# Attention with a gated feed-forward block: one shifted array of the bit-made exponentials goes from VectorE to GpSimd, with a new rule for the number of summed groups

## The chip, the cores and the metric

The kernel runs on one core of a Trainium2 chip. The metric is the device time of one execution in microseconds (us). Three runs of the kernel before gave 769.53, 769.68 and 769.78 us, a median of 769.68.

Five engines matter. TensorE (PE) multiplies matrices into the PSUM banks. ScalarE (ACT) computes the exact exponentials. VectorE (DVE) evicts PSUM banks and makes a second kind of exponential. GpSimd (POOL) has some clearing to do at the start and then rests. SyncE (SP) issues most of the transfers.

## The reference

```python
g = sigmoid((x * gate_w).sum(-1, keepdims=True))       # x: 2048 x 512
q, k, v = split(x @ wqkv)                              # 32 heads of 16
p = softmax(q @ k.T * 16 ** -0.5)                      # 2048 x 2048 for each head
a = concat(p @ v) @ wo
b = (silu(x @ w_gate) * (x @ w_up)) @ w_down           # 1792 columns between
out = g * a + (1 - g) * b
```

The bulk of it is the softmax: 32 heads of 2048 x 2048 exponentials.

## The kernel before

**Tiles.** A unit is 512 queries of four heads; there are 32 of them, and each meets 16 tiles of 128 keys. That makes 512 tiles, numbered n. A tile is four score matrices of 128 keys x 512 queries, one for each head of the unit.

**Two ways to an exponential.** A tile that goes to ScalarE (`emit_pair`, L704) takes two pairs: TensorE writes two heads' scores into a two-bank buffer `s_t` (there are two of these buffers), ScalarE's Exp reads them and writes `e_t`, 128 x 1024 in bf16. A tile that goes to VectorE (`emit_d`, L774) is made from bits. TensorE writes one head's scores into a bank `d_t`; where it can, that matmul runs beside a score pair of ScalarE's ("riding"). VectorE evicts the bank with one multiply and one add into 16-bit integers (`first`, L788). Those integers, read as bf16, are a piecewise linear approximation of the exponential. Four evictions fill an array `c_t` of 128 x 2048 for the four heads; call it y.

**Two corrections.** The approximation is evened out in one of two forms, and `groups[n]` says which. With two groups, VectorE makes two arrays from y with bit operations (`bits`, L825) and multiplies one of them by y (`product`, L834). With four groups, VectorE makes three more arrays by adding 25, 56 and 94 to the integers of y (`SHIFTS`, `copy`, L817). The softmax sum then runs over all arrays of the tile, so that TensorE does the product with V ("PV", `pv`, L902) once for each group: two or four times for a tile of VectorE's, once for a tile of ScalarE's. A PV group is four matmuls that stand side by side in the array, one a head, all into the accumulator `o_ps`.

**Where the arrays live.** Seven places ("homes", `NS`) hold the arrays y and their shifted or masked copies: six tiles of the pool `vex`, and a seventh that is room in `wd_t` early and in `kaug` later. `take_home` picks the one that comes free first, `drop` gives it back once its last reader is planned.

**Around it.** The projections, the feed-forward block and the output products are cut into pieces that TensorE takes between the score pairs.

**What sets the order.** The program is written out by a planner in Python, as it is built. It keeps a clock for TensorE, VectorE and ScalarE (`plan.pe`, `plan.dve`, `plan.act`), adds assumed costs, and always emits the work that fits next. Each engine then runs its instructions strictly in that order (`ordered`, L152), and semaphores hold it where data is late. `v_unit` (L1444) and `v_take` (L1461) decide when VectorE takes a tile away from the end of the unit; ScalarE has the rest (`hi[un]`). `quad` (L1469) decides on two or four groups: two where fewer than two homes are free, four where TensorE had spare time (`spare`) or where `EAGER` holds, else two. Before, `EAGER` never holds. Margins of the plan are constants: `m_free` (L361) lets a bank be reused 0.2 us after its planned eviction, and `d_wait` (L807) plans an eviction 0.28 us after its matmul.

Of the kernel before, what the change touches and what calls it, by code (L numbers as in the profile page):

```python
# [9 lines left out]
ALU = mybir.AluOpType  # L10
AX = mybir.AxisListType
BF16 = mybir.dt.bfloat16
F32 = mybir.dt.float32
U16 = mybir.dt.uint16
# [65 lines left out]
def kernel(  # L80
# [12 lines left out]
    nc = tc.nc  # L93
    P = 128
# [9 lines left out]
    KT = S // P  # L104
    QBW = 512
    QB = S // QBW
# [11 lines left out]
    NV = 4  # L118
    NS = 7
# [5 lines left out]
    SHIFTS = (25.0, 56.0, 94.0)  # L125
# [15 lines left out]
    vex = ctx.enter_context(tc.tile_pool(name="vex", bufs=1))  # L141
# [21 lines left out]
    def mm(*args, **kw):  # L163
        return ordered(nc.tensor.matmul(*args, **kw))  # L164
# [12 lines left out]

    vec = Ordered(nc.vector)
    queue = Ordered(nc.sync)


    xT = big.tile([P, DC, S], BF16, name="xT")
    wd_t = big.tile([P, FC, D], BF16, name="wd_t")
# [36 lines left out]
    kaug = big.tile([P, G, S], BF16, name="kaug")  # L220
# [66 lines left out]


    class Plan:
        pe = dve = act = 0.0  # L290
        mode = last = None
        seq = 0
        slot = -1
# [2 lines left out]
    plan = Plan()  # L296
    owed = []
    work_at = []
    banks = [0.0] * 3
    held = [None] * 3  # L300

    def spend(mode, mms, ready=0.0):

        plan.seq += 1
        work_at.append((plan.pe, mms))
        plan.pe = max(plan.pe + (FLIP if mode != plan.mode else 0.0), ready) + (0.226 if mode == "F" else 0.217) * mms
        plan.mode = mode
# [40 lines left out]
    def m_tile(name, ride=None):  # L348
        while m_ready() is None:
            stuck()  # L350
        i = min((i for i in range(3) if banks[i] is not None), key=lambda i: banks[i])
        if ride is None:
            plan.pe = max(plan.pe, banks[i])
        else:
            ride.append(max(plan.pe - ROUND, banks[i]) + ROUND)
            plan.pe = max(plan.pe, ride[0])
        banks[i] = None
        held[i] = ps_m[i].tile([P, QBW], F32, tag=f"m{i}", name=name)
        return held[i]

    def m_free(ps, t):  # L361
        i = [h is ps for h in held].index(True)
        banks[i], held[i] = t + 0.2, None

    def emit_piece(c):
        mms, f = c.pieces[c.i][:2]
# [313 lines left out]
    c_free = [0.0] * NS  # L680
# [3 lines left out]
    vready = []  # L684
# [15 lines left out]
    e_end = {}  # L700
# [38 lines left out]
    d_wait = []  # L739
# [9 lines left out]
    def drop(i, t):  # L749
        u = users[i]  # L750
        u[:] = u[0] - 1, max(u[1], t)
        if not u[0]:
            c_free[i] = u[1]

    def take_home():
        i = min(range(NS), key=lambda i: c_free[i])
        t, c_free[i] = c_free[i], 1e9
        assert t < 1e9
        users[i] = [1, 0.0]
        return i, t  # L760

    def home(i=None, t=0.0):

        if i is None:
            i, t = take_home()
        plan.dve = max(plan.dve, t)
        if i < NS - 1:
            return i, vex.tile([P, NV * QBW], U16, tag=f"h{i}", name="c_t", bufs=1)[:, :]
        return i, (kaug[:, 0, :] if au > QB else wd_t[:, 0:4, :].rearrange("p f d -> p (f d)")).bitcast(U16)

    ROUND = 0.217
    BANK_WAIT = 0.2
# [1 line left out]
    def emit_d(i, rows=32, riding=False):  # L774
        if not vcur:
            n = v_take()
            waiting[n] = [NV, None, take_home()]
            vcur.update(n=n, left=list(range(NV)), y=None)
            y_live[0] += 1
        n, left, cur = vcur["n"], vcur["left"], waiting[vcur["n"]]  # L780
        left.remove(i)
        end = []
        d_t = m_tile("d_t", end if riding else None)
        score(d_t[:, :], 4 * n + i, rows)
        if not left:
            vcur.clear()

        def first():  # L788
            if cur[1] is None:
                cur[1] = home(*cur[2])  # L790
            h, y = cur[1]
            vec.tensor_scalar(out=y[:, i * QBW:(i + 1) * QBW], in0=d_t[:, :], scalar1=EXP_A, scalar2=EXP_B[groups[n]],
                              op0=ALU.mult, op1=ALU.add)
            m_free(d_t, plan.dve)
            cur[0] -= 1
            if cur[0]:
                return
            plan.last = ("y", n)
            if groups[n] == 2:
                vops.extend([(0.6, lambda: bits(n, 0, y), ("y", n), n, True), (0.6, lambda: bits(n, 1, y), None, n, True),  # L800
                             (MUL_US, lambda: product(n, h, y), None, n, False)])
            else:
                users[h][0] = 2
                ready(n, 0, h, y)
                for k in range(1, 4):
                    vops.append((0.6, lambda k=k: copy(n, k, h, y), ("y", n) if k == 1 else None, n, True))
        d_wait.append(((end[0] if end else plan.pe) + 0.28, first, n))  # L807

    waiting = {}
    copies = {}  # L810
    part = {}

    def ready(n, k, h, c):
        copies[n, k] = (c.bitcast(BF16), h)
        vready.append((plan.dve + 0.3, n, k))

    def copy(n, k, i, y):  # L817
        h, c = home()
        vec.tensor_scalar(out=c, in0=y, scalar1=SHIFTS[k - 1], scalar2=None, op0=ALU.add)
        ready(n, k, h, c)  # L820
        if k == 3:
            drop(i, plan.dve + 0.2)
            y_live[0] -= 1

    def bits(n, k, y):  # L825
        h, c = home()
# [75 lines left out]
    def pv(n, k=None, most=QBW):  # L902

        un = n // KT
        c0 = cut.pop("done", 0)
        c1 = min(QBW, c0 + most)
        cols = slice(c0, c1)
        if un not in o_of:
            while un and un - 1 not in osbs:
                pay()  # L910
            plan.pe = max(plan.pe, o_end[0])
            o_of[un] = ps_o.tile([P, QBW], F32, tag="o", name="o_ps")
        if v_of(n) is not None:
            force(v_of(n))
        o = o_of[un]
        first = pvs[un] in ((0, KT // 2) if un == 0 else (0,))
        last = un == 0 and pvs[un] == KT // 2 - 1 or pv_left(un) == 1
        if k is not None:
            c, slot = copies[n, k]
        for i, b in enumerate(range(4 * n, 4 * n + 4)):  # L920
            j = HEADS[i]
            v0 = (4 * UNIT[un][1] + j) * VC
            e = e_of[b] if k is None else c[:, i * QBW:(i + 1) * QBW]
            mm(o[32 * j:32 * j + 32, cols], lhsT=vaug[:, n % KT, v0:v0 + 32], rhs=e[:, cols],
               start=first, stop=last, tile_position=(0, 32 * j), skip_group_check=True)
        share = (c1 - c0) / QBW
        if c1 < QBW:
            cut.update(item=(n,) if k is None else (n, k), done=c1)
            spend("C", share, 0.0 if k is not None else max(e_end[b] for b in range(4 * n, 4 * n + 4)))
            return  # L930
        cut.clear()
        if k is not None:
            copies.pop((n, k))
        else:
            for b in range(4 * n, 4 * n + 4):
                e_of.pop(b)
                e_left.pop(b, None)
        pvs[un] += 1
        if un == 0 and pvs[0] == KT // 2:
            later(0.6, take_part, plan.pe + 0.47)  # L940
        spend("C", share, 0.0 if k is not None else max(e_end.pop(b, 0.0) for b in range(4 * n, 4 * n + 4)))
        if k is None:
            done_a[un] += 1
        else:
            done_v[un] += 1
            drop(slot, plan.pe + 0.2)
# [187 lines left out]

    plan.act = plan.pe
    plan.dve = plan.pe + 3.9


    pace = Pacer()
# [57 lines left out]
    def v_of(n):  # L1197

        return v_rest[n - QB * KT] if QB * KT <= n < QB * KT + KT else None
# [4 lines left out]
    for qb in range(1, QB):  # L1204
        d = qb * KT
        q, bd = q0_pieces(qb)
        q = pace.add(q, 0, d - 13, [known])
# [3 lines left out]
    for qb in range(QB):  # L1211
        for b in range(NB):
            d = UNIT.index((qb, max(2 * b, 1))) * KT
# [17 lines left out]
            q = pace.add(q_pieces(qb, b), rel, d - QLEAD, after)  # L1231
# [16 lines left out]
    for pos, qb in enumerate(ORDER):  # L1248
# [13 lines left out]
        for tq in range(TQ):  # L1262

            def cond(qb=qb):
                return qb == QB - 1 or all((qb, b) in normed for b in range(NB))
            rel = 100 if pos == 0 else (UNIT.index((qb, G - 1)) + 1) * KT + 16
            c = pace.add((out_pieces if pos else down_pieces)(qb, tq), rel, a0 + per * (0.64 + 0.36 * (tq + 1) / TQ),
                         (gus if tq == 0 else prev) + gates, cond=cond)
# [10 lines left out]
    au = at_ = half = begun = 0  # L1279
    vu = 0  # L1280
    hi = [KT] * UNITS
# [155 lines left out]
    TILE_US = 1.9  # L1437
# [23 lines left out]
    def v_take():  # L1461
        un = v_unit()
        hi[un] -= 1
        n = un * KT + hi[un]
        groups[n] = 2 if quad() else 4
        forward()
        return n

    def quad():  # L1469
        if sum(f < 1e9 for f in c_free) < FREE4:  # L1470
            return True
        if spare[0] > SPARE or EAGER(len(GQL()), back[0]):
            spare[0] = 0.0
            return False
        return True
    FREE4 = 2
    EAGER = lambda q, b: False
    GQL = lambda: []
    back = [0]

# [10 lines left out]
    while au < UNITS:  # L1491
# [10 lines left out]
        if room > 0.02:  # L1502
# [3 lines left out]
            c = side(room + SLACK)  # L1506
# [30 lines left out]
        n = au * KT + at_  # L1537
# [7 lines left out]
    while closed < UNITS or vops or vcur:  # L1545
# [9 lines left out]
        c = side(2.0)  # L1555
# [20 lines left out]
    un = UNITS - 1  # L1576
# [17 lines left out]
    for tq in range(TQ):  # L1594
        t = (QB - 1) * TQ + tq
# [39 lines left out]
```

## Time and profile before

| | us or count |
|---|---|
| median of three runs | 769.68 |
| the profiled execution's own time | 769.63 |
| its span, first to last instruction | 767.9 |
| busy: PE / DVE / ACT / POOL | 733.1 / 738.8 / 752.5 / 10.6 |
| Exp of pairs on ScalarE | 780 (390 tiles) |
| evictions of `d_t` on VectorE | 488 (122 tiles) |
| passes over 128 x 2048 integers on VectorE | 288 |
| products over 128 x 2048 on VectorE | 78 |

780 pairs are 390 tiles of ScalarE's; 488 evictions are the other 122. Of these, 78 have two groups (each has two passes and a product) and 44 have four (three passes each): 2 x 78 + 3 x 44 = 288 passes. The groups of rows in the profile are split by the name of the buffer, so that passes and evictions that write to or read from the seventh home appear under `kaug` or `wd_t`. The mean duration of a row counts each instruction from its start to its end; consecutive instructions overlap, so the busy time divided by the count is the better price of one more. All three big engines are busy for over 95% of the span. The granted clock of TensorE is 1.000 throughout.

### The profile page before, as it was taken

How to read it: one execution, taken by the hardware profiler on the slowest of the kernel's cores; microseconds unless marked ns; L12 is line 12 of the kernel's file. 1: busy time of each engine (PE TensorE's matmuls, PEld its weight loads, DVE VectorE, ACT ScalarE, POOL GpSimd, SP SyncE). 2: the span in 40 equal slices, each digit the busy share in tenths (PEclk: the TensorE clock that was granted, in tenths of full speed). 3: DMA queues.
4: the chain of work that ended last, by engine and by line, in shares of the span. 5: the costliest groups of instructions: out<-in, count | busy, mean ns of one | idle time of the engine just before them, and what ended most of it. 6: DMA issues, size and time to landing. Idle time of an engine off the chain costs nothing.

```text
span 767.9 us, 22047 instructions
## 1 busy us (share of the span) xinstructions
PE 733.1 (95%) x9044; PEld 221.6 (29%) x9045; DVE 738.8 (96%) x1213; ACT 752.5 (98%) x849; POOL 10.6 (1%) x25
## 2 busy tenths in 40 slices
PE   8999999999999999999999999999999999999997
PEld 3323222222222222223322222223222322222222
DVE  6889999999999999999999999999999999999994
ACT  5999999999999999999999999999999999999996
POOL 5000000000000000000000000000000000000000
PEclk9999999999999999999999999999999999999999
DMA  8002304134200113220100230311000232100001
GB/s 192 2 5 50 73 15 85 31 107 101 57 19 13 32 24 78 60 52 22 37 26 12 49 84 20 75 34 41 20 12 26 60 77 59 31 16 16 16 28 35
DMA packets 91020, 34.38 MB, mean 45 GB/s; under 512 B 75488, under 2 KB 90472, under 8 KB 90920
## 3 DMA queue, kind: packets, MB, share of 16 engines
q1 hardware_dynamic: 89192, 32.66, 17.8%
q8 instruction: 70, 1.15, 0.6%
q10 hardware_dynamic: 1728, 0.33, 0.2%
q14 instruction: 30, 0.25, 0.1%
HBM read 21.55 MB, written 2.35 MB: 31 GB/s over the span
## 4 chain that ended last, share of the span: by engine, by line
ACT 32%; PE 30%; DVE 28%; issue 8%; DMA 1%; SPq 1%; DVEq 0%; ACTq 0%
ACT e_t L167 30%; DVE c_t L176 17%; PE s_t L164 10%; PE o_ps L164 8%; PE gu L164 6%; DVE kaug L176 3%; PE ops L164 3%; DVE mt L176 2%; DVE gs L176 2%; ACT th L167 1%; DVE on L176 1%; PE qp L164 1%; DVE osb L176 1%; PE warm L164 1%; SPq L176 1%
## 5 line engine op out<-in xcount | busy, mean ns | idle before, releaser
L167 ACT ACTIVATE e_t<-s_t 128x1024 bf16<-128x1024 f32 x780 | 728.3, 1105 | 1.3 <-PE s_t L164 0.7
L176 DVE TENSOR_SCALAR c_t<-d_t 128x512 uint16<-128x512 f32 x420 | 275.3, 681 | 2.2 <-PE d_t L164 2.0
L164 PE MATMUL s_t<-qx,kaug 32*128 32x512 bf16 (+1 forms) x1228 | 239.0, 384 | 16.1 <-ACT e_t L167 14.0
L164 PEld LDWEIGHTS <-kaug 32*128 32x128 bf16 (+1 forms) x2048 | 88.7, 91 | 321.8 <-issue 317.6
L164 PE MATMUL o_ps<-e_t,vaug 128*32 128x512 bf16 (+2 forms) x1608 | 154.2, 379 | 0.0
L176 DVE TENSOR_SCALAR c_t<-c_t 128x2048 uint16<-128x2048 uint16 x212 | 142.0, 683 | 1.7 <-PE o_ps L164 1.4
L164 PE MATMUL d_t<-qx,kaug 32*128 32x512 bf16 x404 | 131.9, 383 | 0.0
L164 PE MATMUL o_ps<-c_t,vaug 128*32 128x512 bf16 (+2 forms) x1244 | 111.3, 370 | 2.6 <-DVE osb L176 2.1
L164 PEld LDWEIGHTS <-vaug 128*32 128x32 bf16 x3048 | 68.8, 94 | 107.2 <-issue 95.2
L164 PE MATMUL gu<-xT,wg 128*32 128x512 bf16 x896 | 73.0, 384 | 0.0
L164 PE MATMUL gu<-xT,wu 128*32 128x512 bf16 x896 | 68.3, 382 | 0.2 <-DVE c_t L176 0.2
L176 DVE TENSOR_TENSOR c_t<-c_t 128x2048 bf16<-128x2048 bf16 x50 | 60.7, 1213 | 0.0
L164 PE MATMUL ops<-wd_t,mt 128*32 128x512 bf16 x672 | 57.5, 382 | 0.0
L164 PE MATMUL s_t<-q,kaug 32*128 32x512 bf16 (+1 forms) x196 | 38.2, 383 | 5.8 <-ACT e_t L167 5.4
L176 DVE TENSOR_SCALAR kaug<-d_t 128x512 uint16<-128x512 f32 x60 | 39.6, 680 | 0.0
L176 DVE SCALAR_TENSOR_TENSOR mt<-gs,gu 128x512 bf16<-128x512 bf16 x56 | 38.1, 680 | 1.5
L176 DVE SCALAR_TENSOR_TENSOR gs<-th,gu 128x512 bf16<-128x512 bf16 x56 | 38.0, 678 | 0.5 <-ACT th L167 0.5
L167 ACT ACTIVATE th<-gu 128x512 bf16<-128x512 f32 x56 | 37.7, 673 | 0.0
L164 PEld LDWEIGHTS <-mt 128*32 128x32 bf16 (+1 forms) x1037 | 24.5, 95 | 28.6 <-issue 22.0
L164 PEld LDWEIGHTS <-wu 128*32 128x32 bf16 x896 | 19.5, 95 | 25.4 <-issue 17.6
L164 PEld LDWEIGHTS <-wg 128*32 128x32 bf16 x896 | 17.8, 94 | 26.0 <-issue 23.2
L176 DVE TENSOR_SCALAR kaug<-c_t 128x2048 uint16<-128x2048 uint16 x33 | 22.5, 681 | 0.1
(141 smaller groups left out, 444.7 us busy)
## 6 DMA issues: line engine op xcount, KB each, us to landing
wg<-in_B_w_gate_dram SPq DMA_DIRECT2D x56, 128.0 KB
wu<-in_B_w_up_dram SPq DMA_DIRECT2D x56, 128.0 KB
on<-osb SPq DMA_DIRECT2D x120, 16.0 KB
rb<-rr SPq DMA_DIRECT2D x15, 128.0 KB
wd_t<-in_B_w_down_dram SPq DMA_DIRECT2D x7, 256.0 KB
qx<-qst SPq DMA_DIRECT2D x96, 16.0 KB
qx<-aq SPq DMA_DIRECT2D x96, 16.0 KB
out_dram<-o_t SPq DMA_DIRECT2D x12, 128.0 KB
```

Source lines behind the costliest of these rows:

```text
L164: return ordered(nc.tensor.matmul(*args, **kw))
L167: ordered(nc.scalar.activation(*args, **kw))
L176: return lambda *a, **kw: ordered(f(*a, **kw))
```

## The change

For a tile of four groups, the planner now asks `g_fits` whether the third shifted array (the one with 94 added) can be made by GpSimd. It can when GpSimd's own planned clock `plan.pool` is at most 2.0 us ahead of VectorE's, homes are free, and there are at least 9.0 us left before the unit's planned end. Then `g_copy` emits one pass over 128 x 2048 on GpSimd, and reserves 6.3 us for it in the plan. The array counts as ready 0.3 us after that. The home of y is given back when both engines have read it. `EAGER` becomes true where the backlog of unmultiplied pairs is at most 4 and GpSimd's clock is at most 1.0 us ahead of VectorE's, so that such tiles take four groups. `plan.pool` starts at 16.0. Three details of the plan come with it: a PV group of VectorE's arrays is planned not to begin before its array is ready, and the two margins become 0.14 and 0.25 us.

```diff
+    gps = Ordered(nc.gpsimd)
...
     class Plan:
-        pe = dve = act = 0.0
+        pe = dve = act = pool = 0.0
...
-        banks[i], held[i] = t + 0.2, None
+        banks[i], held[i] = t + 0.14, None
...
                 users[h][0] = 2
                 ready(n, 0, h, y)
-                for k in range(1, 4):
+                todo[n] = 3
+                last = 3
+                if g_fits(n):
+                    last = 2
+                    g_copy(n, h, y)
+                for k in range(1, last + 1):
                     vops.append((0.6, lambda k=k: copy(n, k, h, y), ("y", n) if k == 1 else None, n, True))
-        d_wait.append(((end[0] if end else plan.pe) + 0.28, first, n))
+        d_wait.append(((end[0] if end else plan.pe) + 0.25, first, n))
+
+    def usable(t, n, k):
+        vready.append((t, n, k))
+        vready.sort(key=lambda v: v[0])
+        ready_at[n, k] = t
...
+    def copied(n, i, t):
+        todo[n] -= 1
+        left_at[n] = max(left_at.get(n, 0.0), t)
+        if not todo[n]:
+            drop(i, left_at.pop(n) + 0.2)
             y_live[0] -= 1
+
+    todo = {}
+    left_at = {}
+    G_US = 6.3
+    G_WAIT = 2.0
+    G_END = 9.0
+
+    def g_fits(n):
+
+        un = n // KT
+        if plan.pool > plan.dve + G_WAIT or min(c_free) > max(plan.pool, plan.dve) + 0.2 or sum(f < 1e9 for f in c_free) < 2:
+            return False
+        if un < au:
+            return False
+        end = plan.act + (hi[au] - at_) * TILE_US + (hi[un] * TILE_US if un > au else 0.0)
+        return plan.dve + G_END <= end
+
+    def g_copy(n, h, y):
+
+        i, t = take_home()
+        c = vex.tile([P, NV * QBW], U16, tag=f"h{i}", name="c_t", bufs=1)[:, :] if i < NS - 1 else last_home()
+        gps.tensor_scalar(out=c, in0=y, scalar1=SHIFTS[2], scalar2=None, op0=ALU.add)
+        plan.pool = max(plan.pool, plan.dve + 0.15, t) + G_US
+        copies[n, 3] = (c.bitcast(BF16), i)
+        usable(plan.pool + 0.3, n, 3)
+        copied(n, h, plan.pool)
...
-            spend("C", share, 0.0 if k is not None else max(e_end[b] for b in range(4 * n, 4 * n + 4)))
+            spend("C", share, ready_at[n, k] if k is not None else max(e_end[b] for b in range(4 * n, 4 * n + 4)))
...
     plan.dve = plan.pe + 3.9
+    plan.pool = 16.0
...
-    EAGER = lambda q, b: False
+    EAGER = lambda q, b: b <= 4 and plan.pool <= plan.dve + 1.0
```

Because the planner writes out the whole order, the program differs from the first pass on, on TensorE, VectorE, GpSimd and in places on SyncE. The instruction counts of the two built programs:

| instructions | before | after |
|---|---|---|
| Exp of pairs (ACT) | 780 | 770 |
| score matmuls `s_t` (PE) | 1560 | 1540 |
| score matmuls `d_t` (PE) | 488 | 508 |
| PV groups of `e_t` (PE, four matmuls each) | 390 | 385 |
| PV groups of VectorE's arrays (PE) | 332 | 384 |
| evictions of `d_t` (DVE) | 488 | 508 |
| passes over 128 x 2048 integers (DVE) | 288 | 265 |
| products over 128 x 2048 (DVE) | 78 | 62 |
| passes over 128 x 2048 integers (POOL) | 0 | 54 |

More of the change, by code (lines that the diff above doesn't have):

```diff
@@ L768, in home @@
             return i, vex.tile([P, NV * QBW], U16, tag=f"h{i}", name="c_t", bufs=1)[:, :]
-        return i, (kaug[:, 0, :] if au > QB else wd_t[:, 0:4, :].rearrange("p f d -> p (f d)")).bitcast(U16)
+        return i, last_home()
     ROUND = 0.217
@@ L804, in first @@
                 ready(n, 0, h, y)
-                for k in range(1, 4):
-                    vops.append((0.6, lambda k=k: copy(n, k, h, y), ("y", n) if k == 1 else None, n, True))
-        d_wait.append(((end[0] if end else plan.pe) + 0.28, first, n))
+                todo[n] = 3
[4 more added lines that the diff above has]
+                for k in range(1, last + 1):
+                    vops.append((0.6, lambda k=k: copy(n, k, h, y), ("y", n) if k == 1 else None, n, True))
+        d_wait.append(((end[0] if end else plan.pe) + 0.25, first, n))
[3 more added lines that the diff above has]
+        ready_at[n, k] = t
+    ready_at = {}
     waiting = {}
@@ L814, in ready @@
         copies[n, k] = (c.bitcast(BF16), h)
-        vready.append((plan.dve + 0.3, n, k))
+        usable(plan.dve + 0.3, n, k)
     def copy(n, k, i, y):
@@ L820, in copy, with last_home @@
         ready(n, k, h, c)
-        if k == 3:
-            drop(i, plan.dve + 0.2)
-            y_live[0] -= 1
+        copied(n, i, plan.dve)
+    def copied(n, i, t):
[3 more added lines that the diff above has]
+            drop(i, left_at.pop(n) + 0.2)
+            y_live[0] -= 1
+    todo = {}
[19 more added lines that the diff above has]
+        copied(n, h, plan.pool)
+    def last_home():
+        return (kaug[:, 0, :] if au > QB else wd_t[:, 0:4, :].rearrange("p f d -> p (f d)")).bitcast(U16)
     def bits(n, k, y):
@@ L940, in pv @@
             later(0.6, take_part, plan.pe + 0.47)
-        spend("C", share, 0.0 if k is not None else max(e_end.pop(b, 0.0) for b in range(4 * n, 4 * n + 4)))
+        spend("C", share, ready_at[n, k] if k is not None else max(e_end.pop(b, 0.0) for b in range(4 * n, 4 * n + 4)))
         if k is None:
```

## The prediction

> **What bounds the kernel now.** I first read the busy time of the engines by stretch of the span; the columns are the stretch, its length, then busy us and instruction count of PE, PEld, DVE, ACT and POOL, the granted clock and the DMAs.
>
> ```profile
> 0.00:24.00 24.00, 20.84 (x197) 8.42 (x198) 15.17 (x44) 15.27 (x19) 10.60 (x25) 1.00 0.68 154
> 24.00:750.00 726.00, 700.09 (x8734) 208.93 (x8731) 715.79 (x1157) 725.46 (x818) 0.00 (x0) 1.00 0.17 41
> 750.00:768.00 18.00, 12.17 (x117) 4.30 (x116) 7.81 (x14) 11.73 (x14) 0.00 (x0) 1.00 0.11 36
> ```
>
> From 24 to 750 us ScalarE is idle for 726.00 - 725.46 = 0.5 us: it sets the end. VectorE is idle for 10.2 us and TensorE for 25.9 us there, GpSimd for all of it. Outside that stretch VectorE is idle for 8.8 + 10.2 = 19.0 us. Next I read who waited for whom (total us, times, longest).
>
> ```profile
> PE s_t L164 <- ACT e_t L167: 20.3, 60, 0.7
> PE gu L164 <- DVE c_t L176: 0.2, 1, 0.2
> ACT e_t L167 <- PE s_t L164: 0.7, 2, 0.5
> ```
>
> TensorE waits for ScalarE to empty a score buffer, hardly ever the other way round, and next to nothing for a VectorE eviction. So a tile taken from ScalarE shortens the kernel as long as the other two can carry it. The prices are in the groups by cost (busy us, mean ns).
>
> ```profile
> L167 ACT ACTIVATE e_t<-s_t 128x1024 bf16<-128x1024 f32 x780 | 728.3, 1105 | 1.3 <-PE s_t L164 0.7
> L176 DVE TENSOR_SCALAR c_t<-d_t 128x512 uint16<-128x512 f32 x420 | 275.3, 681 | 2.2 <-PE d_t L164 2.0
> L176 DVE TENSOR_SCALAR c_t<-c_t 128x2048 uint16<-128x2048 uint16 x212 | 142.0, 683 | 1.7 <-PE o_ps L164 1.4
> L176 DVE TENSOR_TENSOR c_t<-c_t 128x2048 bf16<-128x2048 bf16 x50 | 60.7, 1213 | 0.0
> ```
>
> An Exp costs 728.3 / 780 = 0.934 us, an eviction 275.3 / 420 = 0.655, a pass over 128 x 2048 integers 142.0 / 212 = 0.670, a product 60.7 / 50 = 1.214.
>
> **The change, part by part.** *ScalarE.* The counts of the built program have 770 Exp for 780: 5 tiles more go to VectorE. 10 x 0.934 = 9.3 us less on the engine that sets the end. This is the whole gain; all else only decides whether it is kept.
>
> *VectorE.* 20 evictions more (+13.1 us), 23 passes fewer (-15.4), 16 products fewer (-19.4): -21.7 us. With its 10.2 us of idle time and a span 9.3 us shorter, 10.2 + 21.7 - 9.3 = 22.6 us stay free, 0.42 us for each of the 54 GpSimd passes. That is the room for whatever GpSimd's presence costs VectorE.
>
> *TensorE.* 52 PV groups more of VectorE's arrays, 5 fewer of ScalarE's, and 10 score rounds fewer. In the timeline, consecutive groups start 0.22 us apart, and about 0.1 us more is lost at each change between scores and PV. That gives +11.4 - 1.1 - 2.2 - 2.0 = +6.1 us. Its idle time in the long stretch falls from 25.9 to 25.9 - 9.3 - 6.1 = 10.5 us. It still fits, but less waiting is left to soak up lateness.
>
> *The GpSimd pass.* No such pass is in the trace of before; its nearest rows are at the start of the span (start, us, instruction):
>
> ```profile
> 2.65 2.29 POOL L266 MEMSET vaug<- 128x512 bf16 x1
> 7.13 1.81 POOL L513 MEMSET qx<- 128x2048 bf16 x1
> ...
> 3.26 0.91 DVE L250 MEMSET kaug<- 128x1024 f32 x1 [0.16 <-issue]
> 7.63 1.29 DVE L176 CAST xT<-tp 128x512 bf16<-128x512 f32 x2 [1.98 <-PE tp L164]
> 14.79 0.91 DVE L176 MEMSET kaug<- 128x1024 f32 x1 [0.16 <-issue]
> ```
>
> The cheap end is 1.81 us: as many elements, written only, in one run. The dear end is the strided clearing, 2.29 us for 512, or 9.2 us for 2048. Between them lies the one GpSimd operation that reads as well as writes, the 0.29 us selection over 128 x 128, which scales to 2.28 ns x 2048 = 4.7 us. I take 4.7, as the pass reads and writes. The plan's own reservation of 6.3 us is a constant in the code, no measurement.
>
> How long may it take? TensorE runs in order, so a PV group on an array that isn't there holds the score matmuls behind it; ScalarE then has at most one filled buffer left, and VectorE's next `d_t` comes late too. In the built program, counted in score pairs between the tile's last `d_t` matmul and the first PV group on GpSimd's array (0.92 us a pair; 47 of the 54 can be told by the array's name), that distance is 7.3 us for 11 passes, 8.3 for 14, 9.2 for 9 and 10.1 to 14.7 for 13. The matmul (0.38 us), the eviction (0.68) and a short start take some 1.3 us of it. So a pass has at least 6.0 us. At 4.7 us it is in time everywhere, and costs the path nothing. If it were not, the price is that of the second rival.
>
> *What the pass does to VectorE.* In the rows above VectorE's clearing takes 0.91 us beside GpSimd's and 0.91 us with GpSimd idle, and two evictions take 1.29 us beside the 1.81 us clearing, no more than elsewhere. Neither of these VectorE instructions reads memory shared with GpSimd's side, though: they write only, or read PSUM. Of VectorE's work in the 6.3 us behind each pass's start, 38% by the built order reads SBUF (passes, products), and in 29 of 54 cases the very next instruction does. The cost of a meeting is bounded below by nothing, as in these rows, and above by the whole length of the pass. I take a value inside the free 0.42 us a pass, because 62% of VectorE's work is of the kind that the rows show undisturbed; that is the step I am least sure of, and its dear end is the first rival.
>
> *The small margins* (0.14 for 0.2 us, 0.25 for 0.28) move matmuls and evictions a little earlier in the order and add no instruction. All waits of TensorE for evicted banks together are under 1 us now; with 0.06 us more on each of 508 evictions the dear end would be 30 us, but a wait that the present margins leave at nearly nothing is more likely to stay there. I take nothing. SyncE's transfers are the same in number.
>
> *The sum.* The profiled execution took 769.6 us (span 767.9, 1.7 us around it), as good as the median of 769.68. 769.6 - 9.3 = 760.3. ScalarE's waits for scores are 0.7 us with TensorE idle for 25.9 us; scaled to an idle time of 10.5 us they become 0.7 x 25.9 / 10.5 = 1.7 us. Forecast: 760.3 + 1.7 = **762.0 us**. Its own range is 758 to 767: a little more than the gain below, some seven tenths of it lost above.
>
> **The rivals.** *First: exclusion for the whole pass (slower).* If a VectorE pass or product can't start while a GpSimd pass runs, VectorE stands still until its end. From the built order, evictions cover the first 0.43 us on average. At 1.81 us a pass that is 54 x 1.38 = 75 us, at 4.7 us 54 x 4.27 = 231 us. VectorE then sets the end: busy 738.8 - 21.7, plus the stall, plus 19.0 idle at the two ends, plus 1.7 around the span: **813 us** and **969 us**. It decides from 0.42 us a pass. For it: VectorE's passes of 128 x 2048 take as long (683 ns) as evictions of a quarter of the elements (681 ns), so they use more of the memory's ports than an eviction does. Against it: nothing in this trace; no two such instructions meet.
> The Trainium skill states this rule: in SBUF — State Buffer, section "Who interferes with whom", VectorE and GpSimd share one port pair, a fast VectorE copy or scalar operation needs it, and whichever starts first holds it for the whole instruction while the other "fully blocks". By that rule the kernel would come out near the times of this rival and not at 762; the rows here neither agree nor disagree, as none has both sides reading.
>
> *Second: the pass takes longer than its place.* If it only yields to VectorE, its time stretches: 4.7 / 0.62 = 7.6 us. Then 11 PV groups come 1.6 us late and 14 come 0.6 us late: 26 us, and 30 us scaled from 47 to 54 passes. TensorE's 10.5 us soak up some; 19.5 us remain: 760.3 + 19.5 = **780 us**. For it: the 38%, and 25 of 47 distances under 9 us. Against: at 1.81 us, 1.81 / 0.62 = 2.9 us is far inside 6.0.
>
> *Third: they take turns.* If each GpSimd pass costs VectorE one pass's time (0.670 us, just what it saves), 54 x 0.670 = 36.2 us stand against the free 22.6; 13.6 us remain: 760.3 + 13.6 = **774 us**.
>
> **How the numbers follow.** Forecast 0.66; first rival 0.16; second 0.09; third 0.07; better than 758 by an effect I don't see 0.02. A difference under 0.2% (1.5 us) can't be told from no change here. Of the forecast's 0.66, 0.02 ends above 768.1, and the second and third rivals may land at half their price (0.02), so same has 0.04; faster is 0.64 + 0.02 + 0.02 (the milder halves of those two rivals) = 0.68; slower 0.28. The range goes from 757 to 790: it holds the forecast and the second and third rivals, 0.82, and leaves out the first rival and the surprise.
>
> **What would show it.** In the profile after: 770 Exp, 54 GpSimd passes of 2 to 6 us each, ScalarE idle for under 3 us between 24 and 750 us, TensorE's waits for `e_t` halved, and no wait of PV groups for GpSimd beyond a few us. VectorE's 128 x 2048 passes stay near 683 ns. If instead their mean or the idle time before them grows, with evictions unchanged, the first or third rival holds; if PV groups wait for GpSimd with VectorE undisturbed, the second. The forecast falls if VectorE is idle or stretched by over 22.6 us more than its own work, or a pass takes over 6 us.

## The result and the profile after

The changed kernel takes 1036.37 us (1035.22 to 1038.19, six runs) beside 769.58 us for the kernel before: a ratio of 1.347, with a 95% interval of 1.346 to 1.349. It is slower by a third. The forecast was 762.0 us and the range ended at 790.

The first lines are the page's busy times of the profiled execution (span 1034.6 us) and its granted TensorE clock in 40 slices.

```profile
PE 839.4 (81%) x9204; PEld 225.0 (22%) x9205; DVE 938.5 (91%) x1194; ACT 763.8 (74%) x839; POOL 311.9 (30%) x79
...
PEclk9898898899889897878887888897898987988988
```

ScalarE, which had been busy for 98% of the span, is down to 74%; VectorE has become the busiest engine. The costliest groups say with what (columns as before: count, busy us, mean ns, idle time before and its releaser):

```profile
L167 ACT ACTIVATE e_t<-s_t 128x1024 bf16<-128x1024 f32 x770 | 735.9, 1048 | 256.6 <-PE s_t L164 166.9
L176 POOL TENSOR_SCALAR c_t<-c_t 128x2048 uint16<-128x2048 uint16 x39 | 218.1, 5591 | 526.4 <-DVE c_t L176 526.4
L176 DVE TENSOR_SCALAR c_t<-d_t 128x512 uint16<-128x512 f32 x432 | 287.6, 686 | 36.1 <-PE d_t L164 33.6
L176 DVE TENSOR_SCALAR c_t<-c_t 128x2048 uint16<-128x2048 uint16 x188 | 269.7, 1448 | 2.4 <-PE o_ps L164 1.6
L176 DVE TENSOR_TENSOR c_t<-c_t 128x2048 bf16<-128x2048 bf16 x42 | 62.2, 1480 | 0.0
```

There are 770 Exp, as counted. A GpSimd pass takes 5.36 us in most cases and 5.58 in the mean of all 54. VectorE's evictions from PSUM take 686 ns, 681 before. But its own passes over 128 x 2048 went from 683 to 1448 ns, and its products from 1213 to 1480. All forms that have grown read SBUF and nothing else; what reads PSUM has kept its length, but for one eviction of 508. The waits show how it travels on (total us, times, longest):

```profile
ACT e_t L167 <- PE s_t L164: 166.9, 84, 5.8
PE o_ps L164 <- DVE c_t L176: 89.6, 27, 5.0
ACT e_t L167 <- PE d_t L164: 87.1, 66, 6.0
```

TensorE's PV groups wait for VectorE's arrays, and ScalarE waits for the scores that stand behind them: 254 us, where it had waited 0.7. No PV group waits for GpSimd in this trace.

Two meetings, in order of time (start us, length us): first GpSimd's rows of the changed kernel, then VectorE's.

```profile
41.07 5.37 POOL L176 TENSOR_SCALAR c_t<-c_t 128x2048 uint16<-128x2048 uint16 x1 [29.46 <-DVE c_t L176]
...
73.69 5.36 POOL L176 TENSOR_SCALAR c_t<-c_t 128x2048 uint16<-128x2048 uint16 x1 [12.58 <-DVE c_t L176]
```

```profile
40.96 0.61 DVE L176 CAST vaug<-vp 128x448 bf16<-128x448 f32 x1
41.49 5.49 DVE L176 TENSOR_SCALAR c_t<-c_t 128x2048 uint16<-128x2048 uint16 x1
46.90 0.67 DVE L176 CAST qst<-qp 128x512 bf16<-128x512 f32 x1
...
74.04 4.35 DVE L176 TENSOR_TENSOR c_t<-c_t 128x2048 bf16<-128x2048 bf16 x1
```

GpSimd begins at 41.07 and ends at 46.44. VectorE's pass, issued at 41.49, ends at 46.98: its own 0.68 us fit in only around the end of GpSimd's. The product issued at 74.04 ends at 78.39, so its own 1.21 us begin at 77.18, 3.49 us into a GpSimd pass of 5.36 that ends at 79.05. (An instruction that was held shows its whole wait in its length; when its own work begins is worked out from its end and its usual length.)

The other meetings in the trace go the same way. 50 of the 54 GpSimd passes hold up one pass or product of VectorE's each: 42 passes, which all end 0.55 us behind GpSimd's, and 8 products, which all end 0.65 us before it. It works in the other direction too: the 23 GpSimd passes that are issued while a VectorE pass or product is under way take 5.44 to 6.27 us, the other 31 take 5.36 to 5.40.

Last, five stretches around the GpSimd pass at 402.31 (stretch, length, busy us of PE, PEld, DVE, ACT, POOL, granted clock, DMA):

```profile
400.00:403.40 3.40, 3.02 (x39) 1.04 (x31) 3.40 (x6) 3.40 (x5) 1.09 (x1) 1.00 0.12 31
403.40:408.00 4.60, 1.08 (x13) 0.31 (x11) 4.60 (x1) 2.84 (x4) 4.28 (x1) 0.98 0.10 25
408.00:411.40 3.40, 2.53 (x22) 0.70 (x25) 3.40 (x6) 0.84 (x1) 0.00 (x0) 0.50 0.51 116
411.40:414.80 3.40, 3.40 (x34) 0.73 (x26) 2.24 (x4) 1.55 (x3) 0.00 (x0) 0.53 0.17 39
414.80:424.00 9.20, 9.20 (x127) 2.57 (x115) 7.95 (x13) 9.01 (x11) 1.29 (x1) 1.00 0.14 32
```

TensorE's first matmuls behind the gap (the bracket has its idle time before them and what ended it):

```profile
408.87 0.62 PE L164 MATMUL o_ps<-c_t,vaug 128*32 128x512 bf16 x4 [4.39 <-DVE c_t L176]
```

While VectorE stands, TensorE runs dry (1.08 us of 4.60 busy); when the work is back, its clock is granted at half for the next 6.8 us. Over the whole span the mean clock is 0.872; the trace's record of the granted clock knows only whole and half, so that it is at half for (1 - 0.872) / 0.5 = 26% of the time. The Trainium skill (TensorE: Matmul & The Clock Gate, Part 1) says that at least one idle window of about 3.4 us takes the array to half its rate, and at least one busy window of that length releases it. The trace agrees: TensorE had stood idle for 4.39 us, and the 6.8 us are two such windows.

### The profile page after: what moved, and what is told of

Its sections match the earlier page's. It is cut to its first block, busy times and chain, and to the rows that moved or that the text cites. A ratio compares the mean times of both kernels' runs of the same rounds, so it can differ in the third digit from the quotient of the medians.

```text
span 1034.6 us, 22438 instructions
## 1 busy us (share of the span) xinstructions
PE 839.4 (81%) x9204; PEld 225.0 (22%) x9205; DVE 938.5 (91%) x1194; ACT 763.8 (74%) x839; POOL 311.9 (30%) x79
## 5 line engine op out<-in xcount | busy, mean ns | idle before, releaser
L176 POOL TENSOR_SCALAR c_t<-c_t 128x2048 uint16<-128x2048 uint16 x39 | 218.1, 5591 | 526.4 <-DVE c_t L176 526.4
L176 DVE TENSOR_SCALAR c_t<-d_t 128x512 uint16<-128x512 f32 x432 | 287.6, 686 | 36.1 <-PE d_t L164 33.6
L176 DVE TENSOR_SCALAR c_t<-c_t 128x2048 uint16<-128x2048 uint16 x188 | 269.7, 1448 | 2.4 <-PE o_ps L164 1.6
L164 PE MATMUL s_t<-qx,kaug 32*128 32x512 bf16 (+1 forms) x1224 | 262.9, 426 | 9.0 <-ACT e_t L167 8.0
L164 PE MATMUL o_ps<-c_t,vaug 128*32 128x512 bf16 (+2 forms) x1380 | 137.1, 420 | 91.0 <-DVE c_t L176 89.6
L164 PE MATMUL d_t<-qx,kaug 32*128 32x512 bf16 x408 | 150.9, 426 | 29.7 <-DVE mt L176 8.0
L164 PE MATMUL o_ps<-e_t,vaug 128*32 128x512 bf16 (+1 forms) x1592 | 164.3, 414 | 0.0
L164 PE MATMUL gu<-xT,wu 128*32 128x512 bf16 x896 | 77.9, 430 | 13.0 <-DVE c_t L176 12.7
L176 POOL TENSOR_SCALAR kaug<-c_t 128x2048 uint16<-128x2048 uint16 x7 | 39.5, 5646 | 91.8 <-DVE c_t L176 86.9
L176 POOL TENSOR_SCALAR c_t<-wd_t 128x2048 uint16<-128x2048 uint16 x4 | 21.5, 5372 | 50.7 <-DVE wd_t L176 29.3
```

The lines of the kernel that those rows point to most:

```text
L176: return lambda *a, **kw: ordered(f(*a, **kw))
```

## The experiments

The theory after the result: a GpSimd pass keeps VectorE from any pass over SBUF until it ends (*exclusion*). Rivals: the new order is too tight for TensorE in itself (*order*), or the array comes too late from GpSimd (*lateness*). All runs stand beside the kernel before on the same chip, 769.0 to 769.2 us in the median.

**1. The same order, but a narrow GpSimd pass.**

```diff
-        gps.tensor_scalar(out=c, in0=y, scalar1=SHIFTS[2], scalar2=None, op0=ALU.add)
+        gps.tensor_scalar(out=c[:, 0:128], in0=y[:, 0:128], scalar1=SHIFTS[2], scalar2=None, op0=ALU.add)
...
+            r = e[:, cols]
+            if k == 3 and n in on_g:
+                r = c[:, 0:P].unsqueeze(1).broadcast_to([P, (c1 - c0) // P, P])
...
```

TensorE reads the 128 columns four times over for each head, so that its work stays the same.

> The order of every engine is that of the changed kernel; only the width of the 54 GpSimd passes goes from 2048 to 128 columns (TensorE reads those 128 columns four times over, so its work is the same; the output is not the reference's). Exclusion theory (a VectorE pass over SBUF stands still until the GpSimd pass ends): a pass of some 0.4 us is over before VectorE's next pass, nothing is left of the loss, and the gain of the 10 Exp shows: 759 to 766 us. Rival, the order itself is too tight for TensorE (52 more PV groups, smaller margins): it stays well above 772 us.

Measured: 762.24 us, ratio 0.991 (0.990 to 0.992). Its busy times, its groups, and the stretch from 24 to 742 us of its span of 760.1:

```profile
PE 735.1 (97%) x9204; PEld 219.0 (29%) x9205; DVE 721.6 (95%) x1194; ACT 744.2 (98%) x839; POOL 50.9 (7%) x79
...
L176 DVE TENSOR_SCALAR c_t<-c_t 128x2048 uint16<-128x2048 uint16 x188 | 127.0, 691 | 0.8
L176 POOL TENSOR_SCALAR c_t<-c_t 128x128 uint16<-128x128 uint16 x39 | 29.3, 750 | 522.0 <-DVE c_t L176 479.7
L176 DVE TENSOR_TENSOR c_t<-c_t 128x2048 bf16<-128x2048 bf16 x42 | 51.3, 1222 | 0.0
```

```profile
24.00:742.00 718.00, 700.66 (x8852) 206.40 (x8854) 697.98 (x1136) 716.30 (x807) 40.25 (x54) 1.00 0.18 42
```

The order is not at fault: with all 770 Exp, all PV groups and the order of every engine as in the changed kernel, and only the width of the 54 GpSimd passes reduced, the kernel is 0.9% faster than before. *Order* falls. VectorE's passes are at 691 ns again, ScalarE is idle for 1.7 us, and the clock is whole.

**2. Half the width.** The same edit with 1024 columns.

> As the run before, with 1024 columns (TensorE reads them twice over; the output is not the reference's). A pass takes some 2.7 us in place of 5.4. Exclusion theory: in the profile of the changed kernel VectorE's blocked instructions start 1.3 us behind the pass's start in 43 of 54 cases; 43 x (2.7 - 1.3) = 60 us of standing still, so 800 to 850 us. Rival, a late array makes TensorE wait: 2.7 us is far inside the 6.0 us that a pass has, so the loss is gone, under 772 us.

Measured: 779.49 us, ratio 1.014 (1.012 to 1.015). *Lateness* falls: the pass takes 3.07 us in the mean, no PV group waits for it, and it still costs 17 us against the narrow one. But the loss is smaller than exclusion until the end would have it, which had given 800 to 850 us. Two GpSimd passes, and VectorE's rows beside the first:

```profile
42.11 2.77 POOL L176 TENSOR_SCALAR c_t<-c_t 128x1024 uint16<-128x1024 uint16 x1 [30.51 <-DVE c_t L176]
...
355.80 2.77 POOL L176 TENSOR_SCALAR c_t<-c_t 128x1024 uint16<-128x1024 uint16 x1 [5.42 <-DVE c_t L176]
```

```profile
42.53 1.16 DVE L176 TENSOR_SCALAR c_t<-c_t 128x2048 uint16<-128x2048 uint16 x1
43.62 0.68 DVE L176 CAST qst<-qp 128x512 bf16<-128x512 f32 x1
```

And the one beside the second:

```profile
358.09 1.02 DVE L176 TENSOR_SCALAR c_t<-c_t 128x2048 uint16<-128x2048 uint16 x1
```

The first VectorE pass ends at 43.69, so its own 0.68 us begin at 43.01, 0.90 us into a GpSimd pass that runs until 44.88. The second, issued at 358.09, 0.48 us before GpSimd's end, ends at 359.11, 0.54 us behind it. So at this width GpSimd holds VectorE off at its start and again near its end, and lets it through between: of the 44 VectorE passes issued beside a GpSimd pass, 15 were let go well before its end, 10 only at its end, and 19 were not held.

**3. The whole width in pieces.** The work is complete again; one instruction becomes 2, 4, 8 or 16. The edit for eight:

```diff
-        gps.tensor_scalar(out=c, in0=y, scalar1=SHIFTS[2], scalar2=None, op0=ALU.add)
+        for p in range(0, NV * QBW, 256):
+            gps.tensor_scalar(out=c[:, p:p + 256], in0=y[:, p:p + 256], scalar1=SHIFTS[2], scalar2=None, op0=ALU.add)
```

> All columns, but each GpSimd pass is cut into four instructions of 512 columns one after the other, some 1.4 us each; the result is the reference's. Exclusion for the length of one instruction: VectorE gets in between the pieces, its longest standstill falls from some 4.6 us to 1.4, TensorE's gaps and half-clock stretches shrink: 850 to 960 us. Exclusion that lasts as long as GpSimd has anything queued: as the changed kernel, 1020 to 1050 us. Rival, a late array: the last piece comes no earlier than before, 1036 us or more.

> All columns, each GpSimd pass in eight instructions of 256 columns; the result is the reference's. If what is left of the loss (13 us with four pieces against the kernel before) is VectorE standing still behind a piece, shorter pieces shrink it: 765 to 779 us. If it is that the array comes later the more pieces there are (the pass of 128 columns took 0.53 us alone, so eight pieces take 7 us or more against the 6.3 that the order allows): 783 us or more, with waits of PV groups for GpSimd.

> The GpSimd pass in two instructions of 1024 columns, the result the reference's, the order of the other engines unchanged. The run with half the columns showed VectorE's passes free again 1.0 us behind the start of a 2.77 us instruction and held again near its end. If an instruction of 1024 columns leaves that opening whatever follows it, two of them cost about twice that run's 20 us of standing still: 790 to 815 us, the granted clock at 0.97 or more. If GpSimd having more queued closes the opening: as the changed kernel, 950 to 1040 us.

> Sixteen pieces of 128 columns, order unchanged. Four pieces lost 20 us against the narrow pass, eight lost 10. If standing still behind a piece goes on shrinking with its length: 764 to 770 us. If the later array (16 x 0.53 = 8.5 us and more, against a mean of 8.75 us for eight) now sets the loss: 773 us or more, with waits of PV groups or of VectorE for GpSimd.

Measured, with the narrow pass of the first run as the floor of this order. The third column is VectorE's busy time above that run's 721.6 us, the fourth the time above its 762.24; the last is how long TensorE's PV groups waited for GpSimd.

| pieces | time (us) | ratio (interval) | VectorE busy | loss | waits for GpSimd |
|---|---|---|---|---|---|
| 1 (the change) | 1036.37 | 1.347 (1.346 to 1.349) | +216.9 | 274.1 | 0 |
| 2 of 1024 columns | 803.33 | 1.044 (1.043 to 1.046) | +45.7 | 41.1 | 0 |
| 4 of 512 | 782.52 | 1.017 (1.016 to 1.019) | +23.6 | 20.3 | 0 |
| 8 of 256 | 772.63 | 1.005 (1.003 to 1.006) | +14.0 | 10.4 | 0.8 |
| 16 of 128 | 825.37 | 1.073 (1.071 to 1.074) | +16.6 | 63.1 | 34.5 |

Four pieces came out below both ranges given for exclusion, which had been worked out from instructions that hold to their end; two and eight came out as expected; sixteen came out where a late array had been expected (773 us or more). From two to eight pieces the loss follows VectorE's added time, at some 0.75 to 0.9 us for each, although GpSimd's work does not shrink: from the start of the first piece to the end of the last the array takes 5.58 us in one piece, 6.5 in two, 7.5 in four and 8.75 in eight. At sixteen it takes 10.7 us. VectorE's added time is close to that of eight pieces, and now lateness makes up most of the loss:

```profile
PE o_ps L164 <- POOL c_t L176: 28.1, 20, 2.6
...
PE o_ps L164 <- POOL kaug L176: 6.4, 5, 2.5
```

**4. Writing only.** GpSimd clears the array and reads nothing.

```diff
-        gps.tensor_scalar(out=c, in0=y, scalar1=SHIFTS[2], scalar2=None, op0=ALU.add)
+        gps.memset(c.bitcast(BF16), 1.0)
```

> The order is that of the changed kernel, but GpSimd clears the array (a memset of 128 x 2048, some 1.8 us, nothing read) where it shifted y; TensorE multiplies that constant, so the output is not the reference's. The clearing no longer waits for y, so it may start earlier. If what excludes VectorE is GpSimd's reading as well as its writing: VectorE's passes (one array in, one out) still stand still for up to 1.8 us, but its products (two arrays in) run at 1213 to 1225 ns as before; 763 to 785 us. If every GpSimd instruction excludes every VectorE instruction over SBUF: products too grow by 0.1 us or more in the mean. If only reading excludes: 759 to 764 us with passes at 690 ns.

Measured: 795.28 us, ratio 1.034 (1.033 to 1.036), 10 us above the range given for this outcome, though the lengths came out as it says. VectorE's busy time is 37.2 us above the narrow run's (758.8 beside 721.6). The groups of this run, and then two meetings, GpSimd's rows before VectorE's:

```profile
L176 DVE TENSOR_SCALAR c_t<-c_t 128x2048 uint16<-128x2048 uint16 x188 | 142.6, 773 | 0.8
...
L176 DVE TENSOR_TENSOR c_t<-c_t 128x2048 bf16<-128x2048 bf16 x42 | 51.0, 1215 | 0.0
```

```profile
177.66 1.80 POOL L176 MEMSET c_t<- 128x2048 bf16 x1 [10.48 <-PE o_ps L164]
...
273.99 1.80 POOL L176 MEMSET c_t<- 128x2048 bf16 x1 [15.92 <-PE o_ps L164]
```

```profile
177.84 2.17 DVE L176 TENSOR_SCALAR c_t<-c_t 128x2048 uint16<-128x2048 uint16 x1
...
273.99 1.22 DVE L176 TENSOR_TENSOR c_t<-c_t 128x2048 bf16<-128x2048 bf16 x1
```

A clearing of 1.80 us holds VectorE's pass until its end (179.46; the pass ends at 180.01), and a product that begins with it takes its usual 1.22 us. Writing alone excludes a pass; a product is excluded only by GpSimd's reading. If GpSimd's reading is over before its writing, that also explains why the products of the changed kernel were let through before the end and the passes only at it; no run here shows the reading and the writing apart. The Trainium skill (SBUF — State Buffer, "Who interferes with whom") states both halves: a fast VectorE pass needs the whole port pair that it shares with GpSimd, an instruction with two SBUF inputs only the pair's read side. Its third statement, that the pair is held for the whole instruction, agrees with VectorE's passes beside 2048 columns. It does not agree with the products there, let go at 3.49 of 5.36 us, nor with the passes beside 1024 columns, where VectorE came through at 0.90 of 2.77 us.

**5. The parts of the change without GpSimd.** First the margins alone, then `EAGER` as well.

```diff
     def g_fits(n):
+        return False
...
-    EAGER = lambda q, b: b <= 4 and plan.pool <= plan.dve + 1.0
+    EAGER = lambda q, b: False
```

The second run has only the first of these two edits.

> The changed kernel with g_fits always false and EAGER always false: no GpSimd pass and the old choice of groups, so that only the two margins and the ready times of the arrays are left of the change. Its built program has 778 Exp for 780: 2 x 0.93 = 1.9 us less on ScalarE. If the margins are harmless: 766.5 to 769.5 us. If 0.06 us less a bank costs waits: 771 us or more.

> The other half of the change alone: EAGER as changed, but g_fits always false, so that all three shifted arrays are VectorE's and four groups are taken wherever the backlog is at most four pairs. The built program has 776 Exp for 780: 4 x 0.93 = 3.7 us less on ScalarE. If the room on TensorE and VectorE carries that: 764.5 to 767.5 us. If TensorE's added PV groups make ScalarE wait: 768 us or more.

Measured: 769.42 us for the margins, ratio 1.0004 (0.9995 to 1.0014), at the top of its range; 769.58 us with `EAGER` as changed, 1.0004 (0.9994 to 1.0013), 2 us above the range for the case that the room carries it. Neither harms, and neither brings what its Exp would. In the second run the last Exp ends at 756.7 us of the span, 759.8 before, but ScalarE's copy of the last accumulator then waits 3.5 us for TensorE, 0.5 us before: what the four Exp gave is lost in the tail. Where the margins' 1.9 us went was not followed.

**6. Attempts at a version that beats both.** GpSimd behind VectorE's own two copies (`sync` from the last copy to the first piece), and plans that reserve more time for the pieces (8.0 us for eight, 9.5 for sixteen).

> Four pieces of 512 columns again, but GpSimd's first piece waits until VectorE's own two copies of the same y are done, so that the VectorE pass that stands right behind the start in 29 of 54 cases is out of the way. The built program has 774 Exp and 50 GpSimd passes. If meetings right behind the start are most of what four pieces lost: 765 to 775 us. If meetings further on are: 776 to 790 us.

> Eight pieces, and the plan reserves 8.0 us for them (G_END 10.5), near the measured 8.75; 43 tiles use GpSimd and the built program still has 770 Exp. If part of the 10 us that eight pieces lost was the array's lateness: 764 to 770 us. If all of it was VectorE standing still: 43/54 of the 10 us remain, 769 to 772 us.

> Sixteen pieces with 9.5 us reserved; 45 tiles use GpSimd, 772 Exp. The narrow pass gave 762 us with 770 Exp; 2 x 0.93 = 1.9 us more is the floor, 764 us. With a few us of standing still: 765 to 769 us, faster than the kernel before. If the plan's room is used up by TensorE and VectorE: 770 us or more.

Measured: 799.18 us (ratio 1.039, 1.037 to 1.040), 777.52 us (1.011, 1.010 to 1.013) and 778.52 us (1.012, 1.009 to 1.014). The first two came out above all their ranges; the third is in the range for a plan without room (770 us or more). With GpSimd behind the copies VectorE's passes take 756 ns, about as with four pieces in front (751), so the later start did not spare VectorE the meetings; and VectorE's evictions now wait 11.4 us for arrays that GpSimd still reads. In the other two the array is hardly late: PV groups wait 0.5 and 3.3 us for GpSimd, where sixteen pieces under the old plan cost 34.5. But all three build another order, whose floor without GpSimd's cost was not measured, so what they lost by can't be told apart. No version in which GpSimd makes the whole array beat the kernel before.

## Why the prediction was wrong

*The gain was right to about 1 us.* 10 Exp less gave 760.3 us, and 1.7 us of waits for ScalarE made it 762.0. The 769.6 us that the sum started from held 0.7 us of these waits already; by its own terms it should have come to 761.3. The narrow pass gave 762.24, with ScalarE idle for 1.7 us of its long stretch. ScalarE's busy time fell by 8.3 us (752.5 to 744.2), not by 9.3, and its idle time in the span grew by 0.5 (15.4 to 15.9), not by 1.0. That 762.0 and 762.24 lie so close is luck; that nearly all of the gain arrives once GpSimd's passes are narrow is not. VectorE's saving was 17.2 us (738.8 to 721.6) rather than 21.7, and TensorE kept 17.3 us of idle time rather than 10.5.

*The length of the pass was off by a fifth and made nothing late.* 4.7 us were taken, 5.58 measured. That is within the 6.0 us allowed, and no PV group waited, so the second rival was not the cause. Its price was also too dear: by the prediction's own distances the 8.75 us of eight pieces would have come some 60 us late in all, and 0.8 us of waiting was measured; the waits came with the 10.7 us of sixteen. Why there was more room than counted was not followed.

*The step that failed* is "What the pass does to VectorE", where a value inside the free 0.42 us a pass was taken "because 62% of VectorE's work is of the kind that the rows show undisturbed". The 62% were indeed undisturbed. But the engine runs in order: one instruction of the other 38% stops all that stands behind it, and one comes soon in nearly every pass. In 50 of 54 passes one was held, issued 1.34 us behind GpSimd's start in the mean. In the changed kernel VectorE loses 216.9 / 54 = 4.0 us a pass, nearly ten times the free 0.42 and six times the third rival's 0.67. A share of time was used where the distance to the first such instruction counted, and a distance of that kind, 0.43 us by the built order, stood in the text of the first rival.

*The room itself was wrong too.* 22.6 us were to be free on VectorE. Eight pieces add 14.0 us to its busy time, and the kernel loses 10.4 us of them. VectorE's idle time is there (718.00 - 697.98 = 20.0 us in the first run) but can't be pooled: a standstill is paid when it happens. I take the reason to be that ScalarE has one filled buffer at most and is the bound, so that what it misses is not made up; the runs show the proportion, not this reason.

*The first rival was the outcome, and too cheap.* It gave 813 to 969 us at a chance of 0.16. By its own formula with the measured 5.58 us, 54 x (5.58 - 0.43) = 278, it would give 1016 us. That this comes near the 1036 measured is luck in part, as it has too much standing still, 278 us where VectorE's busy time grew by 216.9, and too little idle time, 19.0 us where the span has 96.1. The difference in span to the narrow pass, 274.5 us, is 216.9 us of VectorE busy longer and 57.6 us of VectorE idle longer. The latter is mostly waiting for a TensorE that starts again late and at half its clock: VectorE's waits for TensorE add up to 83 us, 27 with the narrow pass. The rival had left that out. How much of the 57.6 us is the clock's alone was not tried.

The Trainium skill's rule (SBUF — State Buffer, "Who interferes with whom") was quoted beside that rival, and said that the kernel would come out near its times. The rival deserved the larger chance: the rows of before held no evidence against it, since no two such instructions met in them.

## What to carry to other kernels

Before moving work to an idle engine, ask which of the busy engine's instructions it would exclude, and how soon the next of these stands in the order; the share of harmless instructions does not tell it where an engine runs in order. Where GpSimd must work beside VectorE's passes over SBUF, give it short instructions: eight pieces cost 10 us where one cost 274, until the pieces' own cost makes the result late. In a program whose order is fixed, count a standstill of a feeding engine as lost for the most part (0.75 to 0.9 us of each here, and more than all of it in the changed kernel, where VectorE also waited for TensorE), not against that engine's total idle time.

## What the hardware showed beyond that

- GpSimd's add on 16-bit integers takes 0.53, 0.84, 1.48, 2.77 and 5.36 us for 128, 256, 512, 1024 and 2048 columns when least disturbed: about 0.2 us and 2.5 ns a column. Clearing 2048 columns takes 1.80.
- It doesn't hold VectorE off throughout when the instruction is short: at 1024 columns VectorE passes came through from 0.90 us on until shortly before the end, at 2048 none did; the products there came through from 3.49 us on.
- Standing still is shown as busy time: a VectorE pass of 0.68 us appears as one of 5.49. A growing mean of one form, with its neighbours unchanged, was the sign.
